# Attention tails turned by TensorE, and an early expert with tiles of its own

## The chip, the cores and the metric

The kernel runs on one core of a Trainium2 chip. The metric is the device time of one execution in microseconds. The kernel before ran three times: 1011.96, 1013.71 and 1017.95 us, a median of 1013.71.

## What is computed

Attention over 8 batches of 8 heads, 576 positions and 64 columns a head. Scores that lie more than tau under their row's maximum count as nothing. Its output, 4608 tokens of 512 columns, goes through a routed layer: a token with a positive skip score is sent to the best of 8 experts, and that expert's result, weighted, is added to it.

```python
scores = scale * np.matmul(q, k.transpose(0, 1, 3, 2))
thresh = np.max(scores, axis=-1, keepdims=True) - tau
scores = np.where(scores >= thresh, scores, -1000000000.0)
attn = np.exp(scores - np.max(scores, axis=-1, keepdims=True))
attn = attn / (np.sum(attn, axis=-1, keepdims=True) + 1e-09)
x = np.matmul(attn, v)                     # then to (4608, 512)
do_compute = x @ w_skip > 0
logits = x[do_compute] @ w_gate;  e_idx = np.argmax(logits, axis=1)
h = np.maximum(xc[mask] @ w1[e], 0.0)      # for each expert e
y[mask] = gate_w[mask, None] * (h @ w2[e])
out = x.copy();  out[do_compute] = xc + y
```

Everything is kept near float32 precision: numbers are split into a high and a low part, and products are made of three matmuls (high by high, high by low, low by high).

## The kernel before

**Attention.** Heads go in 32 pairs. The 576 rows of a head are four blocks of 128 and a tail of 64. A pair has four chunks of two score units each (128 rows by 576 columns) and a ninth unit, M, that holds the tails of both heads, 64 rows and 64 rows. A unit runs as a chain: PE writes scores into one of three PSUM tiles (`sps`, SPB = 3, L522), DVE takes the maximum (L534), ACT makes the threshold (L541) and the exponential (L546), DVE multiplies with the mask (L554), which gives p and frees the PSUM tile. ACT copies p to float16 (L336, "hi"), POOL subtracts to get the low half (L603), and SP issues two DMA transposes of 128-blocks (L608), one of the high and one of the low half. PE multiplies the turned p with v (L643, "AV", tile `avp`). The tail's p (`pm`, one buffer) goes the same way through `hm` and `TM`, five blocks to a transpose instead of nine.

After two chunks and after the tail, ACT copies the AV result to `a`; z, the divisors, is made by DVE (L681, reciprocal L684); POOL scales (L693, L706); PE transposes the result in float32 into the one tile `gps` (GPB = 1, L749), ACT copies it (`xf`), and PE makes the gate's logits (L775; L836 for tails). Every two batches a gate (from L854 on) ranks the tokens of an expert (L938, L939) and POOL scatters the tokens' records into lists (L997).

**What sets the order.** All of this is written out by a list scheduler (class Plan, L77 to L178). Each operation has a key, its place n in the sequence plus an entry of the table OFF (L73), a set of engines with a cost, and dependencies. A ring (`ring.take`, `ring.free`) limits the buffers. Each engine takes, of the operations that are ready by the planner's own costs, the one with the smallest key. The result is one fixed order for each engine; at run time engines wait for each other by semaphores.

**The passage.** One expert, the "early" one, is picked after the last but one batch. While the last attention goes through PE, POOL gathers its tokens (L325), PE transposes them (L1170), ACT and DVE split them into `xh` and `xl` (L1179, L1183), and layer 1 makes eight groups of 12 matmuls (L1204), each followed by ACT's relu (L1207) and DVE's low half (L1210). The four transposes and eight groups all use the tile `gps`. `QK0` and `QK1`, in which `xh`, `xl` and the results lie, use the memory of `hla` and `PTa`. The last logits and tails use score tiles instead. SP reads the lists into `recs` (L1225, L1231).

**The experts.** A loop over jobs (L1611), that is over pieces of an expert's list. For each, POOL gathers tokens from `out` (L325 from L1379), PE transposes them (L1394), makes layer 1 (L1412) and layer 2 (L1474, L1493). Weights are split by ACT (L1374) and by DVE and POOL (L1375). DVE adds the result to the token (L1451), and POOL scatters the rows to `out` (L1452).

Of the kernel before, what the change touches and what calls it, by code (L numbers as in the profile page):

```python
# [73 lines left out]
    ld=1.2, qs=-97.2, S=24.7, mx=-53.4, th=-79.8, e=-1.0, p=-17.9, ph=-22.6, pl=-42.8, tt=40.9, av=108.8, cp=11.0, x=122.9, xw=-26.7, row=49.6, rsp=68.9, init=47.1, L1=20.1, sc=-81.4, d0=88.6, phD=-79.0, v=51.0, vsp=6.9, V2=25.9,  # L74
# [107 lines left out]
def attn_moe_kernel(ctx: ExitStack, tc: tile.TileContext, qq, kk_, vl, vt, tau, wg, w1, w2, out):  # L182
# [43 lines left out]
    XWD = (NFT + NDT) * CAPE  # L226
# [4 lines left out]
    QZs = [a1.tile([P, 2 * S], F32, name=f"QZ{i}") for i in range(QB)]  # L231
    hls = [hla[:, i] for i in range(HLB)]
# [4 lines left out]
    hms = [a1.tile([P, STEP + 1, P], F16, name=f"hm{i}") for i in range(2)]  # L237
# [22 lines left out]
    def settle_m():  # L260
        for hm in hms:
            hv = hm.rearrange("p (a c) n -> p a (c n)", a=2)
            nc.gpsimd.memset(hv[:, :, S:], 0.0)

    ones16 = cp.tile([P, P], BF16, name="ones16")
    linit = cp.tile([P, NB, 2], F32, name="linit")
# [241 lines left out]
    def plan_chunk(g, i):  # L508
# [34 lines left out]
        def expo(u):  # L543
            T["e", g, i, u] = e = ap_.tile([P, 2, HS], F32, name="e", tag="e", bufs=EB)
            c = 2 * i + u
            nc.scalar.activation(e, bank(u), AF.Exp, bias=T["mx", g][:, 0, c : c + 1])  # L546

        def mask(u):
            if M:
                T["p", g, i] = ap_.tile([P, 1, S], F32, name="pm", tag="pm", bufs=1)  # L550
# [24 lines left out]
        for u in units:  # L575
            take = [(ks[0],)] if u else ring.take("pm", 1) if M else ring.take("p", PFB)
# [3 lines left out]
            ks.append(k)  # L580
        if M:
            ring.free("kt", T["Sop", g])
            ring.free("qz", T["Sop", g])
            ring.free("mx", ks)

        def fph():
            if M:
                T["hl", g, i] = hms[g % 2].rearrange("p a b -> p (a b)")
                T["PT", g, i] = TMs[g % 2]
            else:  # L590
                c = NM * g + i
                T["hl", g, i] = hls[c % HLB]
                T["PT", g, i] = PTs[c % PTB]
# [4 lines left out]
        lo0 = (NM + 1) * P if M else w  # L598
# [20 lines left out]
        plan_av(g, i, n, [t0, t1])  # L619

    def plan_av(g, i, n, pt):
# [5 lines left out]
        def av():  # L627
# [22 lines left out]
            n + OFF["av"], av, pt + T["V", b, hp // 2] + T["settle"][1:2] + prev + ([] if prev else ring.take("avp", 1)),  # L650
# [8 lines left out]
    def plan_out(g, i, n):  # L659
        b, hp = divmod(g, HP)  # L660
        M = i == NM
        k = n + OFF["cp"]
# [23 lines left out]
        k = n + OFF["x"]  # L686
        zz = pl.op(k, fz, [x, T["a0"]] + ring.take("z", 4), {DVE: 0.09})
# [35 lines left out]
        k = n + OFF["x"] + 1  # L723
# [37 lines left out]
    def plan_logits(b, hp, k):  # L761
# [3 lines left out]
        t, x = plan_x(k, (b, hp), T["xm", b, hp], lambda t: T["x", b][:, t, hp * P : (hp + 1) * P], last)  # L765
        T["xr", b, hp] = t
        js = []
        for j in range(2):

            def mm(j=j):  # L770
                if j == 0:
                    ps = T["Z", (b, hp)][:, 1] if last else g_tile().rearrange("p a b -> p (a b)")
# [7 lines left out]
            held = [] if last else ring.take("gps", GPB)  # L780
# [12 lines left out]
        ring.free("sps" if last else "gps", [y])  # L793
        if hp == HP - 1:
            if b == B - 2:
                plan_gate(k + 2, pr, 0, NM, [y])
# [20 lines left out]
    def plan_tails(b, k, xtm):  # L817
# [9 lines left out]
        t, x = plan_x(k, ("t", b), xtm, lambda d: T["x2"][:, d * P : (d + 1) * P], last)  # L827
        ring.free("x2", [t, s])
        js = []
        for j in range(2):  # L830

            def mm(j=j):
                if j == 0:
                    T["lvt"] = T["Z", ("t", b)][:, 1, 0:16] if last else g_tile()[:, 0, 0:16]
# [5 lines left out]
            held = [] if last else ring.take("gps", GPB)  # L840
# [8 lines left out]
        ring.free("sps" if last else "gps", [y])  # L849
# [174 lines left out]
    kk = cp.tile([P, 2, E, E], F32, name="kk")  # L1024
# [51 lines left out]
    def plan_early(k, j):  # L1076
# [97 lines left out]
        def xh(d):  # L1174
            if d == 0:
                QKs[:] = [ep.tile([P, XWD], F32R, name=f"QK{i}", tag=f"QK{i}") for i in range(2)]
                j.hh, j.hl = (q[:, 0:nh].rearrange("p (f n) -> p f n", n=CAPE) for q in QKs)
                j.xh, j.xl = (q[:, nh : nh + nx] for q in QKs)
            nc.scalar.activation(j.xh[:, d * CAPE : (d + 1) * CAPE], T["x0", d][:, 0:CAPE], AF.Copy)  # L1179

        def xl(d):
            xs_ = slice(d * CAPE, (d + 1) * CAPE)
# [4 lines left out]
        for a in range(NDT):  # L1187
            t = pl.op(k2 + a, lambda a=a: xt(a), gs + ring.take("gps", GPB), {PE: 0.108 * j.nb})
            q = xo[-2:-1] if a else list(T["last"])
            xo.append(pl.op(k2 + a + 0.1, lambda a=a: xh(a), [t] + q, {ACT: 0.4}))  # L1190
            q = xo[-2:-1] if a else []
            xo.append(pl.op(k2 + a + 0.2, lambda a=a: xl(a), xo[-1:] + q, {DVE: 0.45}))
            ring.free("gps", xo[-1:])
        for f in range(NFT):
# [19 lines left out]
            y = pl.op(k2 + 1 + 0.5 * f, mm, xo[-2:] + hs + ls + ring.take("gps", GPB), {PE: 12 * 0.136})  # L1214
            y = pl.op(k2 + 1.3 + 0.5 * f, hh, [y], {ACT: 0.42})
# [539 lines left out]
```

## Time and profile before

| | value |
|---|---|
| median of 3 runs | 1013.71 us (1011.96 to 1017.95) |
| the profiled execution's own time | 1010.29 us |
| its span, first to last instruction | 1008.5 us |
| mean granted clock of PE | 0.933 of full |
| PE busy | 837.2 us, 83% |
| PE's weight loads (beside the matmuls) | 719.3 us, 71% |
| DVE, ACT, POOL busy | 674.4, 609.9 and 593.4 us |
| DMA queue of transposes, loads and stores | 76.0% of 16 engines' span |

The span has three stages, which the rows below cut at 664 and 732 us. Busy shares are of the whole span; how an engine stands in a stage is seen in the stage's own row. A wait is the idle time of an engine just before an instruction, with what ended it in brackets. [...]

### The profile page before, as it was taken

To read this page: it belongs to the slowest core of one execution; us is meant where nothing else is said; L and a number is where in the kernel's file an instruction comes from. 1 tells how busy PE (TensorE), PEld (TensorE's weight loads), DVE (VectorE), ACT (ScalarE), POOL (GpSimd) and SP (SyncE) were. 2 spreads that over 40 slices of the span, in tenths; PEclk is the share of its full clock that TensorE was granted. 3 is DMA by queue.
4 is the path that set the end of the run, shared out by engine and by line. 5 is a ranking of instruction groups with operands and counts; after the bars stand their busy time and mean duration, and the time that the engine had idled before them with its cause. 6 is when DMAs were issued, how large, how long until landed. Compare 5 with 4: busy or idle time off the path is not lost. (4 is left out here: it accounts for less than half of the span.)

```text
span 1008.5 us, 21609 instructions
## 1 busy us (share of the span) xinstructions
PE 837.2 (83%) x8274; PEld 719.3 (71%) x8274; DVE 674.4 (67%) x1143; ACT 609.9 (60%) x1020; POOL 593.4 (59%) x398
## 2 busy tenths in 40 slices
PE   6788988878889877897988789856697999977985
PEld 5677767757668766776876677645576899967974
DVE  6888878788787787876767878982134565526431
ACT  4778968856787965796886588641123344334430
POOL 3667767748776864686684488763025464445251
PEclk9999999989999997998999899975998999988998
DMA  6999999999999999899999899993046543453420
GB/s 161 185 193 183 190 222 178 195 210 173 177 206 186 199 221 179 152 188 200 172 173 226 162 159 200 158 206 129 2 147 207 188 168 128 152 187 114 160 83 17
DMA packets 387656, 169.89 MB, mean 168 GB/s; under 512 B 354615, under 2 KB 355383, under 8 KB 387552
## 3 DMA queue, kind: packets, MB, share of 16 engines
q1 hardware_dynamic: 382928, 158.35, 76.0%
q0 software_dynamic: 4480, 10.15, 3.1%
q8 instruction: 66, 1.08, 0.4%
q14 instruction: 38, 0.31, 0.1%
q10 hardware_dynamic: 144, 0.00, 0.0%
HBM read 67.76 MB, written 15.21 MB: 82 GB/s over the span
## 5 line engine op out<-in xcount | busy, mean ns | idle before, releaser
L522 PE MATMUL sps<-kt,QZ 128*128 128x288 f32 (+2 forms) x1408 | 353.1, 400 | 70.3 <-DVE p L554 58.8
L603 POOL TENSOR_TENSOR hla<-p,hla 128x1152 f16<-128x1152 f32 x128 | 305.1, 2385 | 162.2 <-ACT hla L336 112.4
L522 PEld LDWEIGHTS sps<-kt,QZ 128*128 128x128 f32 x1408 | 248.9, 201 | 120.6 <-issue 57.4
L534 DVE TENSOR_REDUCE mx<-sps 128x1 f32<-128x576 f32 x288 | 215.3, 752 | 113.3 <-PE sps L522 111.8
L546 ACT ACTIVATE e<-sps,mx 128x576 f32<-128x576 f32 x288 | 205.5, 730 | 29.6 <-DVE mx L534 25.6
L554 DVE SCALAR_TENSOR_TENSOR p<-sps,mx,e 128x576 f32<-128x576 f32 x256 | 197.8, 807 | 13.9 <-POOL hla L603 5.3
L643 PEld LDWEIGHTS <-PTa 128*128 128x128 f16 x3840 | 140.6, 101 | 52.0 <-DMA PTa<-hla 28.9
L643 PE MATMUL avp<-Vh,PTa 128*128 128x65 f16 x2560 | 145.4, 198 | 33.6 <-DMA PTa<-hla 24.5
L336 ACT ACTIVATE hla<-p 128x1152 f16<-128x1152 f32 x128 | 148.5, 1161 | 32.0 <-DVE p L554 15.5
L643 PE MATMUL avp<-Vl,PTa 128*128 128x64 f16 x1280 | 137.5, 196 | 0.0
L541 ACT ACTIVATE mx<-mx,ntau 128x2 f32<-128x2 f32 (+1 forms) x160 | 47.0, 294 | 78.8 <-DVE mx L534 77.1
L1375 POOL TENSOR_TENSOR wl<-wr,wh 128x1024 fp32r<-128x1024 f32 x28 | 72.0, 2589 | 22.8 <-ACT wh L1374 18.3
L1412 PE MATMUL hps<-xh,wh 128*128 128x288 f32 (+4 forms) x224 | 69.1, 308 | 0.1
L1412 PE MATMUL hps<-xl,wh 128*128 128x288 f32 (+4 forms) x224 | 68.0, 304 | 0.0
L1412 PE MATMUL hps<-xh,wl 128*128 128x288 f32 (+4 forms) x224 | 67.8, 303 | 0.0
L1452 POOL DMA_INDIRECT out<-o,ids x20 | 20.0, 1000 | 80.0 <-DVE o L1451 25.1
L1413 ACT ACTIVATE QK<-hps 128x288 fp32r<-128x288 f32 (+4 forms) x56 | 23.9, 426 | 61.0 <-PE hps L1412 60.3
L1374 ACT ACTIVATE wh<-wr 128x1024 fp32r<-128x1024 f32 x60 | 60.6, 1050 | 0.0
L1474 PE MATMUL yps<-wh,QK 128*128 128x512 f32 (+2 forms) x224 | 57.1, 405 | 1.7 <-ACT wh L1374 1.5
L325 POOL DMA_INDIRECT xg<-out,idg x20 | 22.6, 1130 | 60.9 <-issue 33.9
L1375 DVE TENSOR_TENSOR wl<-wr,wh 128x1024 fp32r<-128x1024 f32 x32 | 46.0, 1445 | 9.6 <-ACT wh L1374 9.3
L997 POOL DMA_INDIRECT lst<-rec,si x36 | 35.9, 998 | 25.1 <-DVE si L969 17.9
(236 smaller groups left out, 1285.8 us busy)
## 6 DMA issues: line engine op xcount, KB each, us to landing
wr<-in_w SPq DMA_DIRECT2D x31, 1024.0 KB, 5.5
kt<-in_k SPq DMA_DIRECT2D x32, 288.0 KB, 3.7
QZ<-in_q SPq DMA_DIRECT2D x64, 144.0 KB, 3.3
vraw<-in_vl SPq DMA_DIRECT2D x32, 256.0 KB, 4.7
out<-xb SPq DMA_DIRECT2D x32, 256.0 KB, 3.4
PTa<-hla SPq DMA_TRANSPOSE x256, 3.8
vraw<-in_vt SPq DMA_DIRECT2D x8, 128.0 KB, 4.5
TM<-hm SPq DMA_TRANSPOSE x64, 2.7
```

The source lines that it names most:

```text
L336: nc.scalar.activation(dst, src, AF.Copy)
L522: nc.tensor.matmul(ps[:, j, o : o + w], q[:, at : at + P], k[:, c0 : c0 + w], start=True, stop=True, skip_group_check=True,)
L534: nc.vector.tensor_reduce(T["mx", g][:, 0, c : c + 1], bank(u), AX.XY, ALU.max, negate=True)
L541: nc.scalar.activation(m[:, 1, cs], m[:, 0, cs], AF.Identity, bias=ntau, scale=-1.0)
L546: nc.scalar.activation(e, bank(u), AF.Exp, bias=T["mx", g][:, 0, c : c + 1])
L554: nc.vector.scalar_tensor_tensor(T["p", g, i][:, u].rearrange("p (a b) -> p a b", a=2), bank(u), T["mx", g][:, 1, c : c + 1], T.pop(("e", ...
L603: nc.gpsimd.tensor_tensor(hl[:, lo0 : lo0 + w], T.pop(("p", g, i)).rearrange("p a b -> p (a b)"), hl[:, 0:w], op=ALU.subtract)
L643: nc.tensor.matmul(o[:, 0:e], x[:, w_, cs], y[:, vb, 0:e], start=first and j == 0, stop=kt == NM and j == 2, skip_group_check=True,)
L1374: nc.scalar.activation(w[0][:, sl], rs, AF.Copy)
L1375: lo[q % 2].tensor_tensor(w[1][:, sl], rs, w[0][:, sl].bitcast(F32), op=ALU.subtract)
L1412: nc.tensor.matmul(hp_[:, 0:cap], w_, x, start=(i == 0), stop=(i == len(mm) - 1))
L1474: nc.tensor.matmul(yp[0:m], h, w_, start=(i == 0), stop=(i == len(mm) - 1))
```

## The change

Four things change, and all numbers of the table OFF are new.

1. The tail's p is written in float32 to one of two fixed buffers (`pms`). PE transposes its five blocks in float32 into a score tile; ACT copies that to float16 as the high half, and DVE subtracts to get the low half. This takes the place of ACT's copy, POOL's subtraction and the two DMA transposes of the tail. The turning of a chunk is written after the next chunk's scores.
2. z is made by ACT instead of DVE. The e tiles lie in one fixed buffer.
3. The early expert has `hh0`, `hl0` and `xh0` of its own, its transposes and layer-1 results use the three score tiles, and layer 1 has a key of its own (`L1m`). The last logits and tails use `gps`.
4. A gather is no longer made to wait for scatters of other tokens, nor a scatter for such gathers.

```diff
 ...
-    hms = [a1.tile([P, STEP + 1, P], F16, name=f"hm{i}") for i in range(2)]
+    ea = a1.tile([P, EB, 2, HS], F32, name="ea", tag="EE")
+    hh0, hl0 = (ep.tile([P, NFT, CAPE], F32R, name=f"h0{i}") for i in range(2))
+    xh0 = a1.tile([P, NDT * CAPE], F32R, name="xh0")
+    pms = [a1.tile([P, (NM + 1) * P], F32, name=f"pm{i}") for i in range(2)]
...
+        return lambda: plan_turn(g, i, n, units, ks)
+
+    def plan_turn(g, i, n, units, ks):
+        if i == NM:
+            plan_tail(g, i, n, ks)
+            return
...
+    def plan_tail(g, i, n, ks):
+        def tr():
+            T["X", g] = ps = ps_s.tile([P, 2, 512], F32, name="sps", tag="sps").rearrange("p a b -> p (a b)")
+            for t in range(NM + 1):
+                nc.tensor.transpose(ps[:, t * P : (t + 1) * P], pms[g % 2][:, t * P : (t + 1) * P], ident)
+        def hi(e):
+            T["PT", g, i] = TMs[g % 2]
+            copy(e, T["PT", g, i][:, 0 : NM + 1].rearrange("p a b -> p (a b)"), T["X", g][:, 0 : (NM + 1) * P])
+        def lo():
+            x = T["PT", g, i]
+            nc.vector.tensor_tensor(
+                x[:, NM + 1 :].rearrange("p a b -> p (a b)"),
+                T.pop(("X", g))[:, 0 : (NM + 1) * P],
+                x[:, 0 : NM + 1].rearrange("p a b -> p (a b)"),
+                op=ALU.subtract,
+            )
+        t = pl.op(n + OFF["tt2"], tr, ks + ring.take("sps", SPB), {PE: 1.15})
+        a = pl.op(n + OFF["hi2"], hi, [t] + ring.take("hmT", 2), {ACT: 0.63})
+        c = pl.op(n + OFF["lo2"], lo, [a], {DVE: 0.76})
+        ring.free("pm", [t])
+        ring.free("sps", [c])
+        plan_av(g, i, n, [a, c])
...
-            nc.vector.tensor_scalar(z, T["a", g][:, :, :, D], 1.0e-9, T["s", b], op0=ALU.add, op1=ALU.mult)
+            nc.scalar.activation(z, T["a", g][:, :, :, D], AF.Identity, bias=T["s9", b], scale=T["s", b])
...
-        nx, nh = NDT * CAPE, NFT * CAPE
+        j.hh, j.hl, j.xh = hh0, hl0, xh0
         def half():
-            return g_tile().rearrange("p a b -> p (a b)")
+            return ps_s.tile([P, 2, 512], F32, name="sps", tag="sps")[:, 0]
...
-            t = pl.op(k2 + a, lambda a=a: xt(a), gs + ring.take("gps", GPB), {PE: 0.108 * j.nb})
+            t = pl.op(k2 + a, lambda a=a: xt(a), gs + ring.take("sps", SPB), {PE: 0.108 * j.nb})
...
-            y = pl.op(k2 + 1 + 0.5 * f, mm, xo[-2:] + hs + ls + ring.take("gps", GPB), {PE: 12 * 0.136})
+            y = pl.op(k2 + OFF["L1m"] + 0.5 * f, mm, xo + hs + ls + ring.take("sps", SPB), {PE: 12 * 0.136})
...
         for t in range(j.nb):
             m = j.m(t)
-            gather(j.xg[0:m, t, :], j.idg[0:m, t : t + 1], NTOK)
+            ga = gather(j.xg[0:m, t, :], j.idg[0:m, t : t + 1], NTOK)
+            for x in rows:
+                tc.declare_no_dep(ga.ins, x.ins, reason="every token goes to one expert")
+            gets.append(ga)
...
-        for x in rows:
+        for x in rows + gets:
             tc.declare_no_dep(sc.ins, x.ins, reason="every token goes to one expert")
```

Line numbers below are those of each kernel: the early expert's transposes are L1170 before and L1202 after, its layer-1 matmuls L1204 and L1233.

On DVE, around the end of a pair in the middle of attention, before: `mx` is the maximum of a unit, `p` the mask, `pm` the tail's mask.

```order
L554 SCALAR_TENSOR_TENSOR p<-sps,mx,e 128x576 x2
L554 SCALAR_TENSOR_TENSOR pm<-sps,mx,e 128x576
L534 TENSOR_REDUCE mx<-sps 128x1
L787 COPY lg<-gps 128x64
L534 TENSOR_REDUCE mx<-sps 128x1 x2
L554 SCALAR_TENSOR_TENSOR p<-sps,mx,e 128x576 x2
L681 TENSOR_SCALAR z<-a_111,vmx 128x10
L684 RECIPROCAL z<-z 128x10
```

The same place after the change:

```order
L556 SCALAR_TENSOR_TENSOR pm_116<-sps,mx,ea 128x576
L536 TENSOR_REDUCE mx<-sps 128x1 x2
L716 RECIPROCAL z<-z 128x10
L556 SCALAR_TENSOR_TENSOR p<-sps,mx,ea 128x576 x2
L638 TENSOR_TENSOR TM_118<-sps,TM_118 128x640
L536 TENSOR_REDUCE mx<-sps 128x1 x3
L556 SCALAR_TENSOR_TENSOR p<-sps,mx,ea 128x576 x2
```

The tail's low half (L638) stands between the masks of a later chunk and three maxima; z is gone from DVE.

On PE, at the end of attention, before: the last logits (L775), the rank of the last gate (L938, L939), then the early expert.

```order
L775 MATMUL sps<-wgt,xf 128x16 x2
L938 LDWEIGHTS tri_120
L938 MATMUL gps<-rs_9706,tri_120 128x8
L939 LDWEIGHTS ones_116
L939 MATMUL gps<-rs_9706,ones_116 128x8
...
L1170 MATMUL gps<-ident,xg_9592 128x128 x2
L1170 MATMUL gps<-ident,xg_9592 128x64
L1170 MATMUL gps<-ident,xg_9592 128x128 x2
```

After, the same engine from the last AV matmul on:

```order
L674 MATMUL avp<-Vh_113,TM_119 64x65
L1202 MATMUL sps<-ident,xg_9406 128x128 x2
L1202 MATMUL sps<-ident,xg_9406 128x64
...
L781 MATMUL gps<-ident,x_7567 128x128 x4
L1202 MATMUL sps<-ident,xg_9406 128x128 x2
L1202 MATMUL sps<-ident,xg_9406 128x64
L869 MATMUL gps<-wgt,xf 128x16 x4
L1233 MATMUL sps<-xh_110,wh_9194 128x320
L1233 MATMUL sps<-xl_9500,wh_9194 128x320
L1233 MATMUL sps<-xh_110,wl_9205 128x320
```

The early expert's transposes and four of the eight groups of layer 1 now stand ahead of the rank of the last gate, mixed with the last logits and tails; the other four stand right behind it.

On POOL, late in the loop over jobs, before: L1452 is a scatter, L325 a gather, and brackets name the semaphores that an instruction waits for (DMASW are queue slots of POOL's own transfers).

```order
L1452 DMA out<-o,ids 4608x512 [waits DVE_49]
L325 DMA xg<-out,idg 128x512 [waits DMASW6_49,DMASW7_49,DMASW0_49,DVE_49]
L325 DMA xg<-out,idg 128x512
L325 DMA xg<-out,idg 32x512
L1375 TENSOR_TENSOR wl<-wr,wh 128x1024 [waits DMAHW1_49,Activation_49]
```

After:

```order
L1507 DMA out<-o,ids 4608x512 [waits DMASW0_49,DVE_49]
L327 DMA xg<-out,idg 128x512 [waits DMASW1_49,DVE_49]
L327 DMA xg<-out,idg 128x512 [waits DMASW2_49]
L327 DMA xg<-out,idg 32x512 [waits DMASW3_49]
L1427 TENSOR_TENSOR wl<-wr,wh 128x1024 [waits DMAHW1_49,Activation_49]
```

The place is the same; the gather waits for one slot, used eight transfers before, instead of three that hold the scatters just ahead of it.

## Rows read from the trace of the kernel before

**Rows 1.** The span by stage: length; PE, PEld, DVE, ACT, POOL busy (instructions); clock, DMA share, GB/s.
```profile
7.00:664.00 657.00, 550.30 (x6512) 462.69 (x6511) 523.74 (x845) 493.38 (x824) 452.30 (x270) 0.95 1.01 186
664.00:732.00 68.00, 39.71 (x299) 33.47 (x296) 25.11 (x71) 15.95 (x32) 18.35 (x17) 0.70 0.38 104
732.00:1008.00 276.00, 242.01 (x1444) 217.96 (x1442) 122.00 (x202) 98.29 (x163) 117.74 (x72) 0.94 0.40 142
```

**Rows 2.** Waits of PE from 7 to 664 us: microseconds in total, times, longest.
```profile
PE sps L522 <- DVE p L554: 58.8, 48, 3.9
PE avp L643 <- DMA PTa<-hla: 21.4, 20, 3.0
```

**Rows 3.** Timeline of the passage: start, duration, engine, line, tiles, idle before.
```profile
692.65 1.01 PE L775 MATMUL sps<-wgt,xf 128*128 128x16 f32 x4
...
705.04 0.90 PE L1204 MATMUL gps<-QK,wh 128*128 128x320 f32 x2 [1.05 <-DVE QK L1183]
...
709.12 0.49 DVE L1210 SCALAR_TENSOR_TENSOR QK<-gps,QK 128x320 fp32r<-128x320 f32 x1 [4.13 <-ACT QK L1207]
...
721.42 0.49 DVE L1210 SCALAR_TENSOR_TENSOR QK<-gps,QK 128x320 fp32r<-128x320 f32 x1 [2.58 <-ACT QK L1207]
...
710.03 5.36 SPq L1231 DMA_DIRECT2D recs<-lst  x7
```

**Rows 4.** Waits of PE from 730 to 1009 us.
```profile
PE yps L1493 <- POOL wl L1375: 11.7, 2, 6.4
```

**Rows 5.** Timeline of POOL at 754 us, and of DVE and POOL from 912 to 936.
```profile
754.02 1.06 POOL L325 DMA_INDIRECT xg<-out,idg  x1 [2.60 <-DMA out<-o,id]
...
923.00 1.22 DVE L1375 TENSOR_TENSOR wl<-wr,wh 128x1024 fp32r<-128x1024 f32 x1 [0.41 <-ACT wh L1374]
...
923.89 1.27 POOL L325 DMA_INDIRECT xg<-out,idg  x1 [5.40 <-DMA out<-o,ids]
...
927.03 7.00 POOL L1375 TENSOR_TENSOR wl<-wr,wh 128x1024 fp32r<-128x1024 f32 x3
```

**Rows 6.** Waits of PE from 664 to 732 us.
```profile
PE gps L1204 <- DVE QK L1210: 7.4, 7, 1.1
```

**Rows 7.** Tile xg: operation, count, ns minimum/median/maximum, first and last start.
```profile
L325 POOL DMA_INDIRECT xg<-out,id x3: 957/1007/1066, 679.7 to 682.4; - x3
```

**Rows 8.** DMA issues from 676 to 700 us: count, median us to landing.
```profile
xg<-out,id POOLq DMA_INDIRECT x3, 5.6
```

**Rows 9.** Stretch of 695 to 700 us.
```profile
695.00:700.00 5.00, 2.19 (x8) 1.07 (x8) 3.63 (x27) 0.48 (x2) 0.00 (x0) 0.50 0.00 2
```

**Rows 10.** Timeline, PE at 317 us and DVE at 755 us.
```profile
317.02 0.63 PE L749 MATMUL gps<-ident,xb 128*128 128x128 f32 x4
...
755.53 0.69 DVE L1444 TENSOR_TENSOR QK<-xtp,QK 128x512 fp32r<-128x512 f32 x1 [5.17 <-ACT QK L1443]
```

**Rows 11.** Groups by line and shape: busy us, mean ns, idle before.
```profile
L603 POOL TENSOR_TENSOR hm<-pm,hm 128x576 f16<-128x576 f32 x32 | 41.7, 1303 | 4.1 <-ACT hm L336 4.1
L541 ACT ACTIVATE mx<-mx,ntau 128x2 f32<-128x2 f32 x128 | 37.6, 294 | 71.2 <-DVE mx L534 70.6 <-DVE vki L443 0.4
...
L681 DVE TENSOR_SCALAR z<-a,vmx 128x10 f32<-128x10 f32 x32 | 30.0, 936 | 4.9 <-ACT a L336 4.9
...
L336 ACT ACTIVATE hm<-pm 128x576 f16<-128x576 f32 x32 | 21.4, 670 | 1.8 <-DVE pm L554 1.8
```

**Rows 12.** Tile TM.
```profile
L608 SPq DMA_TRANSPOSE TM<-hm x64: 1200/1247/2872, 32.1 to 675.4; - x64
```

**Rows 13.** The page's costliest groups.
```profile
L522 PE MATMUL sps<-kt,QZ 128*128 128x288 f32 (+2 forms) x1408 | 353.1, 400 | 70.3 <-DVE p L554 58.8
```

**Rows 14.** DMA queues from 100 to 600 us: packets, MB, share.
```profile
q1 hardware_dynamic: 276474, 93.54, 100.6%
```

**Rows 15.** Tile PTa from 100 to 600 us.
```profile
DMA to landing us min/median/max: 3.2/3.7/6.9
```

**Rows 16.** The page's HBM line.
```profile
HBM read 67.76 MB, written 15.21 MB: 82 GB/s over the span
```

More of the change, by code (lines that the diff above doesn't have):

```diff
@@ L543, in expo @@
         def expo(u):
[L544 removed]
+            T["e", g, i, u] = e = ea[:, (STEP * g + 2 * i + u) % EB]
             c = 2 * i + u
@@ L580, in plan_chunk @@
             ks.append(k)
+        T["masks"] = T.get("masks", [])[-2:] + ks
         if M:
@@ L680, in fz @@
             T["z", g] = z = ap_.tile([P, NM + 1, 2], F32, name="z", tag="z", bufs=4)
-            nc.vector.tensor_scalar(z, T["a", g][:, :, :, D], 1.0e-9, T["s", b], op0=ALU.add, op1=ALU.mult)
+            nc.scalar.activation(z, T["a", g][:, :, :, D], AF.Identity, bias=T["s9", b], scale=T["s", b])
         def fr():
             nc.vector.reciprocal(T["z", g], T["z", g])
-        k = n + OFF["x"]
-        zz = pl.op(k, fz, [x, T["a0"]] + ring.take("z", 4), {DVE: 0.09})
+        k = n + OFF["x"] - late_
+        zz = pl.op(k, fz, [x, T["a0"]] + ring.take("z", 4), {ACT: 0.2})
         zz = pl.op(k + 0.1, fr, [zz], {DVE: 0.11})
@@ L778, in mm @@
                     )
-            held = [] if last else ring.take("gps", GPB)
+            held = ring.take("gps", GPB)
             js.append(pl.op(k + 1 + 0.5 * j, mm, [x, T["init"]] + (held if j == 0 else js), {PE: 0.43}))
@@ L792, in plan_logits @@
         T["lgo", b] = y = pl.op(k + 1.8, lg, deps, {DVE: 0.135})
-        ring.free("sps" if last else "gps", [y])
+        ring.free("gps", [y])
         if hp == HP - 1:
             if b == B - 2:
+                k -= OFF["eg"]
                 plan_gate(k + 2, pr, 0, NM, [y])
@@ L838, in mm @@
                     )
-            held = [] if last else ring.take("gps", GPB)
+            held = ring.take("gps", GPB)
             js.append(pl.op(k + 1 + 0.5 * j, mm, [x, T["init"]] + (held if j == 0 else js), {PE: 0.43}))
@@ L848, in plan_tails @@
         T["lgt", pr] = y = pl.op(k + 1.8, lg, js + [T["lgo", b - 1]], {DVE: 0.1})
-        ring.free("sps" if last else "gps", [y])
+        ring.free("gps", [y])
     cnt_op = []
@@ L1174, in xh @@
         def xh(d):
[L1175 to L1178, printed above, removed]
             nc.scalar.activation(j.xh[:, d * CAPE : (d + 1) * CAPE], T["x0", d][:, 0:CAPE], AF.Copy)
         def xl(d):
+            if d == 0:
+                j.xl = a1.tile([P, NDT * CAPE], F32R, name="xl0", tag="EE")
             xs_ = slice(d * CAPE, (d + 1) * CAPE)
@@ L1292, in op @@
             return pl.op(k, lambda: None, deps, eng, lat=lat)
-        hs = [op([T["w2"][q // 2]], {ACT: 0.947}) for q in range(4)]
-        ls = [op([x], {DVE: 1.135}) for x in hs]
+        hs = [op([T["w2"][q // 2]] + [(y,) for y in T["hh"]], {ACT: 0.947}) for q in range(4)]
+        ls = [op([x] + [(y,) for y in T["L1"]], {DVE: 1.135}) for x in hs]
         x = op([T["list"]] + [(y,) for y in ls], {DVE: 0.2})
@@ L1354, in attn_moe_kernel, with tile @@
     ps_y = moe.enter_context(tc.tile_pool(name="ps_y", bufs=3, space=PSUM, reuse_waits="tile"))
-    late = moe.enter_context(tc.tile_pool(name="late", bufs=1))
+    class late:
+        at, base = 0, None
+        @classmethod
+        def tile(cls, shape, dt, name):
+            if cls.base is None:
+                cls.base = ep.tile([P, NFT * CAPE], F32, name="lateb", tag="h00")
+            n = int(np.prod(shape[1:]))
+            x = cls.base[0:1, cls.at : cls.at + n]
+            cls.at += n
+            if len(shape) == 3:
+                return x.rearrange("p (a b) -> p a b", a=shape[1])
+            if len(shape) == 4:
+                return x.rearrange("p (a b c) -> p a b c", a=shape[1], b=shape[2])
+            return x
     tab = cp.tile([1, 2 * NOV + 1], I32, name="tab")
@@ L1359, in attn_moe_kernel @@
     rows = []
+    gets = []
+    QKs[:] = [ep.tile([P, NFT * CMAX], F32R, name=f"QK{i}", tag=f"QK{i}") for i in range(2)]
     def split_w(src, raws=(), lo=(nc.vector, nc.gpsimd)):
```

72 lines of the change are left out of this document (36 added, 36 removed).

## The prediction

> **What bounds the kernel now.** I read the table of stages first. It cuts the span into attention (7 to 664 us), the passage from attention to the experts (664 to 732) and the experts (732 to 1008) [rows 1]. In attention PE is busy 550 of 657 us at a mean clock of 0.95, DVE 524, ACT 493, POOL 452, and the DMA share is 1.01: four engines are loaded between 69 and 84%, none is full. In the passage PE is busy 40 of 68 us at a clock of 0.70 and every other engine less: that stretch is a chain of dependent steps. In the experts PE is busy 242 of 276.
>
> Next, PE's own waits in attention [rows 2]: 58.8 us for a score tile that DVE's mask still reads, 21.4 us for transposed p to land. The first is the ring of three score tiles, the second the way over DMA. Then the passage by instructions [rows 3]: logits until 693.66, layer 1 of the early expert from 705.04, then one of its eight groups every 3.07 us ((721.42 - 709.12) / 4). Last, PE's wait in the experts for the low halves of the weights [rows 4], and on POOL the gathers ahead of these halves [rows 5].
>
> **The early expert (first term).** Before, its four transposes and eight groups of 12 matmuls share one PSUM tile and stand behind the last gate. Of the 3.07 us of a group PE waits 7.4/7 = 1.06 us for DVE to empty the tile [rows 6]. With three tiles PE writes the next one meanwhile, so a group costs it 3.07 - 1.06 = 2.01 us, and eight cost 16.1.
>
> The start moves too: transposes and layer 1 stand right behind the last AV matmuls, ahead of the last rank. The three gathers that they need are issued by 682.4 + 1.0 and land 5.6 us after issue, about 689 [rows 7, 8]. I take 690 for the start. To the 16.1 us come 3 for logits, tails and rank that are now mixed in (three groups of four small matmuls, 1.01 us each at half clock [rows 3]), and 3.2 for a start at half clock. The granted clock is 0.50 from 695 to 700 [rows 9], and the first group, begun in that state, took 709.12 - 705.04 = 4.08 us from its first matmul to DVE's reading, where a later one takes about 2.5 (3.07 less DVE's 0.49 and some 0.08 until PE starts again). That is 1.58 a group; I count two. End: 690 + 16.1 + 3 + 3.2 = 712.3. Before, the eighth group ends three periods after the fifth, 721.42 + 3 x 3.07 - 0.5 = 730.1. The difference is 17.8; I take **-18**. Bounds: no group at half clock, -21; all eight, six more by 1.58 = 9.5 later, -8.
>
> Layer 2 is let follow as before. What could be late next is the gather of the first listed job, which needs the lists: SP issues their reads until 710.03 + 5.36 = 715.4 [rows 3], about when layer 1 is now done, and layer 2 lies between that gather and its use.
>
> From 695 to 700 PE had float32 transposes and small gate matmuls, at a granted 0.50 [rows 9], and attention, which holds four float32 transposes per pair already, a mean of 0.95 [rows 1]. [...]
>
> **Gathers (second term).** POOL's gather of a job waits for the scatter of the job before, which writes other tokens. The gather at 923.89 sat 5.40 us for it, and three low halves of weights queue behind it, from 927.03 [rows 5]. DVE's first half starts at 923.00, when ACT's first piece is there; ACT needs about 1 us for the next, so POOL could start near 924: 3.1 us earlier, 3.5 with the gathers' slack. Of this pattern there are three; at the other two the same working gives 4.2 each. PE waits 11.7 us for such halves at two of them [rows 4], so the gain reaches it. The first gather of the loop, at 754.02, sat 2.60, and PE waits for what it brings. Sum 3.5 + 4.2 + 4.2 + 2.6 = 14.5; since PE may meet its next wait sooner, I take **-13**. Bounds: 0, if queue slots or lists hold the gathers instead; -18, the three waits of PE (11.7, and about 4 at the third) with the 2.6.
>
> **Attention (third term).** Per pair, 32 times:
> - PE: four float32 transposes take 0.63 us [rows 10], so the five that are added 0.78, in all 25 us. PE is idle 657 - 550 = 107 us of this stage, so a part falls into waits: I count half, +12. Best 0, worst +25.
> - PE's wait for transposed p: ten DMA transposes per pair become eight, and the tail's AV needs no DMA. Of the 21.4 us and some 6 that I add for the tail's own, half goes: **-14**.
> - POOL: the low half of the tail goes, 41.7 us [rows 11]. POOL is idle a third of the stage, so alone it is worth nothing.
> - ACT: the copy of 576 columns goes (0.67 each), one of 640 comes, 0.67 x 640/576 = 0.74, and z comes, priced like the nearest small row at 0.29 [rows 11]: 32 x 0.36 = +12 on 493. Hidden in its 164 us of idle time; if not, +12 is inside the bounds.
> - DVE: z goes, 30.0 us [rows 11] (a mean with stalls in it), and the low half of 640 columns comes, 0.69 x 640/512 = 0.86 [rows 10], 27.6: about -2.
> - SP: 64 issues of 1.25 us go, 80 us of its queue [rows 12]; what this is worth is rival 1.
> - Score ring: nine allocations a pair become ten. The tile is held for transposes, ACT's and DVE's copy, 0.78 + 0.74 + 0.86 = 2.4 us and latencies. Nothing, if that falls beside other units; at worst PE loses a score unit per pair, 353.1/288 = 1.23 us [rows 13], 39 us.
>
> The added DVE step stands between two masks and the transposes behind the first scores of the next pair, so PE and DVE have other work around them; that cover is why I take 0 for the ring. Sum: +12 - 14 = **-2**, bounds +40 (about PE's worst and half the ring) and -40 (rival 1).
>
> For a larger gain speaks the queue with the transposes: 100.6% of 16 engines' time [rows 14]. Against it, a transpose lands 3.2/3.7/6.9 us after issue (minimum, median, maximum) [rows 15], so no backlog grows, and HBM moves 82 GB/s over the span [rows 16]. [...]
>
> **Sum.** -18 - 13 - 2 = -33. The profiled execution took 1010.3 us (span 1008.5 and 1.8 around it), which gives 977.3. The median of the runs lies 3.4 above that execution: **980**. Own range 966 to 994: first two terms between -39 and -8, not both at one end, attention 10 either way.
>
> **Rivals.**
> 1. The transposes' queue, or SP that issues into it, paces attention. A pair has 72 blocks of other transposes and 10 of the tail's: 10/82 of 657 us is 80, half of it 40. 980 - 38 = 942. For it: the share in rows 14 and the 80 us of SP. Against: rows 15, and that PE's longest wait is for the mask. Chance 0.13.
> 2. PE pays in full. For it: PE is the most loaded engine, and its order is fixed, so a transposition that waits for a late mask holds up the scores behind it. Attention +20: 980 + 22 = 1002, still faster. Against: the 107 us of idle time. Chance 0.15.
> 3. The passage gains little, because layer 2 or the first listed job meets a new wait (lists, weights, clock): first term -5, gathers -6, attention +10. 1013.7 - 1 = about 1013. For it: the lists come no earlier. Against: layer 1's groups lose their wait wherever they stand. Chance 0.08.
> 4. Slower: the tenth tile in the ring of three. Each pair loses a score unit, 1.23, on top of the 0.78: 32 x 2.01 = 64, less the 31 of the first two terms, 1013.7 + 33 = 1047. From 31/32 = 0.97 us per pair on, the kernel is slower. For it: the 58.8 us of rows 2 are a wait for this ring. Against: it is one tile in ten, emptied by copies and not by the chain of maximum, exponential and mask. Chance 0.09.
>
> Forecast 0.55. Times of this kernel can be told apart from about 0.5% on, 5 us. Faster: 0.55 + 0.13 + 0.15 = 0.83; same 0.08; slower 0.09. The range 946 to 1008 leaves out rivals 3 and 4 and half of rival 1, about 0.2.
>
> **What would show it.** Right, if layer 1's groups stand about 2 us apart and end near 712, gathers follow scatters without the 5 us, PE's waits for POOL's halves go below 2 us each, and attention keeps its length within 10 us. The ring shows as PE's wait for score tiles far above 59 us; the queue as an attention some 40 us shorter; rival 2 as PE's busy time up by 25 with its waits unchanged. I am wrong if attention moves by more than 15 us, or if the clock stays at 0.5 through layer 1.

## The result and the profile after

The changed kernel takes 938.66 us, the median of four runs (935.18 to 942.50), against 1012.84 for the kernel before beside it: a ratio of 0.927, with an interval of 0.921 to 0.933. The forecast was 980, with a range of 946 to 1008: the sign was right, the size was not, and the time lies under the range. The profiled execution has a span of 935.8 us, 72.7 less than before.

Three marks divide that: the start of the last AV matmul (685.6 before, 649.2 after), the first matmul of layer 2 of the early expert (731.59 and 679.03), and the end.

| | before | after | difference | forecast |
|---|---|---|---|---|
| attention, to the last AV | 685.6 | 649.2 | -36.4 | -2 |
| passage, to layer 2 | 46.0 | 29.8 | -16.2 | -18 |
| experts, to the end | 276.9 | 256.8 | -20.1 | -13 |

The stretches of the changed kernel, with the columns of [rows 1]:

```profile
7.00:649.00 642.00, 559.48 (x6821) 481.47 (x6820) 533.56 (x863) 511.62 (x869) 426.51 (x247) 0.97 0.94 180
649.00:679.00 30.00, 24.14 (x142) 21.63 (x139) 10.38 (x48) 8.72 (x20) 7.42 (x9) 0.82 0.29 103
679.00:935.00 256.00, 238.21 (x1444) 214.67 (x1444) 139.43 (x202) 98.64 (x163) 120.03 (x73) 0.97 0.45 153
```

and attention of the kernel before, cut at its own last AV:

```profile
7.00:686.00 679.00, 562.18 (x6670) 473.55 (x6669) 537.65 (x865) 500.65 (x837) 464.24 (x279) 0.94 1.01 189
```

PE was given 160 transposes (23.0 us) and is still busy 3 us less, at a mean clock of 0.97 instead of 0.94; its idle time fell from 116.8 to 82.5 us. Its waits in the changed kernel, which answer to [rows 2], from 7 to 645 us:

```profile
PE sps L524 <- DVE p L556: 53.7, 50, 3.4
PE avp L674 <- DMA PTa<-hla: 6.3, 10, 1.7
```

The wait for turned p fell from 21.4 to 6.3 us. The wait for the score ring is no longer than before (58.8), so the tenth tile did not do the harm that rival 4 feared; a smaller cost can't be ruled out by this row, since other things changed with it.

The passage, PE's timeline after, which answers to [rows 3]:

```profile
653.44 0.48 PE L1202 MATMUL sps<-ident,xg 128*128 128x128 f32 x1 [4.02 <-DMA xg<-out,id]
654.30 2.60 PE L1202 MATMUL sps<-ident,xg 128*128 128x128 f32 x8 [0.39 <-DMA xg<-out,id]
656.83 1.12 PE L781 MATMUL gps<-ident,x 128*128 128x128 f32 x4
657.74 0.93 PE L1202 MATMUL sps<-ident,xg 128*128 128x128 f32 x3
658.64 1.89 PE L869 MATMUL gps<-wgt,xf 128*128 128x16 f32 x8
660.37 0.61 PE L1233 MATMUL sps<-xh,wh 128*128 128x320 f32 x1
660.78 0.47 PE L1233 MATMUL sps<-xl,wh 128*128 128x320 f32 x1
661.04 0.47 PE L1233 MATMUL sps<-xh,wl 128*128 128x320 f32 x1
...
666.98 0.31 PE L1233 MATMUL sps<-xh,wl 128*128 128x320 f32 x1
667.13 0.30 PE L1233 MATMUL sps<-xh,wh 128*128 128x320 f32 x1
...
677.25 0.31 PE L1233 MATMUL sps<-xh,wl 128*128 128x320 f32 x1
679.03 4.04 PE L1529 MATMUL yps<-wh,h 128*128 128x512 f32 x16 [1.47 <-ACT wh L1426]
```

Layer 1 runs from 660.37 to 677.56, 17.2 us instead of 25, with no wait between groups. The matmuls stand 0.26 us apart in the first group and 0.15 later: one group at half clock (granted 0.52 from 660.0 to 663.6 us and 1.00 from there to 677.56), where two were counted. It starts 11 us after the last AV and not 4 as assumed. The wait of 4.02 us for the gathered tokens was foreseen. Behind it stand 4.0 us of the tokens' own transposes (L1202), at a mean granted clock of 0.51 from 653 to 660, and 3.0 us of logits and tails (L781, L869).

### The profile page after: what moved, and what is told of

Same layout as the page of the kernel before. It is cut to its first block, busy times and chain, and to the rows that moved or that the text cites. A ratio compares the mean times of both kernels' runs of the same rounds, so it can differ in the third digit from the quotient of the medians.

```text
span 935.8 us, 21710 instructions
## 1 busy us (share of the span) xinstructions
PE 827.0 (88%) x8434; PEld 722.9 (77%) x8434; DVE 686.9 (73%) x1140; ACT 621.2 (66%) x1054; POOL 559.2 (60%) x367
## 5 line engine op out<-in xcount | busy, mean ns | idle before, releaser
L524 PE MATMUL sps<-kt,QZ 128*128 128x288 f32 (+2 forms) x1408 | 340.8, 392 | 59.6 <-DVE p L556 53.7
L524 PEld LDWEIGHTS sps<-kt,QZ 128*128 128x128 f32 x1408 | 245.1, 196 | 107.8 <-issue 44.3
L548 ACT ACTIVATE ea<-sps,mx 128x576 f32<-128x576 f32 x288 | 207.7, 731 | 27.4 <-DVE mx L536 15.9
L556 DVE SCALAR_TENSOR_TENSOR p<-sps,mx,ea 128x576 f32<-128x576 f32 x256 | 196.6, 810 | 14.0 <-ACT mx L543 10.9
L674 PEld LDWEIGHTS <-PTa 128*128 128x128 f16 x3840 | 135.8, 100 | 21.8 <-DMA PTa<-hla 9.6
L674 PE MATMUL avp<-Vh,PTa 128*128 128x65 f16 x2560 | 139.8, 196 | 10.9 <-DMA PTa<-hla 7.9
L674 PE MATMUL avp<-Vl,PTa 128*128 128x64 f16 x1280 | 132.8, 194 | 0.0
L1427 DVE TENSOR_TENSOR wl<-wr,wh 128x1024 fp32r<-128x1024 f32 x32 | 52.1, 1642 | 7.9 <-ACT wh L1426 7.8
L487 POOL TENSOR_TENSOR Vl<-vraw,Vh 128x1024 f16<-128x1024 f32 (+1 forms) x23 | 44.6, 1939 | 9.4 <-ACT Vh L338 9.3
L1469 DVE SCALAR_TENSOR_TENSOR QK<-hps,QK 128x288 fp32r<-128x288 f32 (+4 forms) x56 | 26.4, 471 | 32.4 <-ACT QK L1468 32.2
```

The costliest lines, as they stand in the source:

```text
L487: (nc.gpsimd if e == POOL else nc.vector).tensor_tensor(T["Vl", b][:, ts], vraw[:, ts], Vh[:, ts, 0:D], op=ALU.subtract)
L524: nc.tensor.matmul(ps[:, j, o : o + w], q[:, at : at + P], k[:, c0 : c0 + w], start=True, stop=True, skip_group_check=True,)
L556: nc.vector.scalar_tensor_tensor(T["p", g, i][:, u].rearrange("p (a b) -> p a b", a=2), bank(u), T["mx", g][:, 1, c : c + 1], T.pop(("e", ...
L674: nc.tensor.matmul(o[:, 0:e], x[:, w_, cs], y[:, vb, 0:e], start=first and j == 0, stop=kt == NM and j == 2, skip_group_check=True,)
L1427: lo[q % 2].tensor_tensor(w[1][:, sl], rs, w[0][:, sl].bitcast(F32), op=ALU.subtract)
```

## The experiments

Each ran beside the kernel before; ratios are to that, and the last AV's start is from the one profiled execution of each. That execution can lie some microseconds from the run's median: 8.0 above it in x3 (969.54 us), 6 to 7 below it in x11 and x15, 4.5 below it in x6. Differences in the last column are uncertain by as much. The diffs show the lines that matter and not the whole edits.

```
run                       us       ratio (interval)        last AV
before                    1010-1013                        685.6
after                     938.66   0.927 (0.921 to 0.933)  649.2
x1_tail_by_dma            985.75   0.968 (0.962 to 0.975)  695.4
x3_old_table              961.58   0.948 (0.946 to 0.951)  678.9
x15_old_table_urgent      964.38   0.954 (0.950 to 0.957)  682.9
x4_z_on_dve               963.98   0.952 (0.950 to 0.955)  672.8
x4c_z_reduce_on_dve       934.50   0.924 (0.920 to 0.929)  651.0
x2_idle_dma               967.35   0.955 (0.953 to 0.957)  678.9
x6_idle_dma_small         961.13   0.953 (0.949 to 0.958)  668.7
x11_idle_plain_dma        958.93   0.949 (0.943 to 0.956)  664.2
x7_before_z_on_act        1000.48  0.991 (0.987 to 0.994)  671.7
x8_before_no_tail_dma     990.83   0.983 (0.978 to 0.988)  663.0
x9_before_both            973.45   0.961 (0.954 to 0.968)  649.0
x5_before_gathers         989.65   0.978 (0.972 to 0.984)  687.3
x10_one_transpose         943.81   0.933 (0.927 to 0.939)  657.6
x12_loads_on_pool         955.89   0.944 (0.940 to 0.949)  670.4
x13_loads_on_act          956.93   0.946 (0.942 to 0.950)  666.1
x14_stores_on_pool        947.16   0.936 (0.933 to 0.940)  655.7
```

### The tail's way, and the order

x1 gives the changed kernel the tail's old way, x3 the old table. z stays on ACT in both, and the turning of a chunk stays behind the next chunk's scores.

```diff
 # x1_tail_by_dma, in plan_tail
+        a = pl.op(n + OFF["ph"], fph, ks + ring.take("hm", 2), {ACT: w / 1200 + 0.12})
+        c = pl.op(n + OFF["pl"], fpl, [a], {POOL: w * 0.00208 + 0.1})
+        t0 = pl.dma(n + OFF["tt"], lambda: turn(0), [a] + ring.take("hmT", 2), [nb * 8 * 0.0193], 0.3)
 # x3_old_table: the numbers of before in OFF, and
+    tt2=95.0, hi2=-20.0, lo2=5.2, eg=0.0, L1m=1.0, ex=0.0, eav=0.0,
```

> The changed kernel, but the tail's p is turned as before (ACT's float16 copy, POOL's low half, two DMA transposes); table, z on ACT, early expert and gathers stay as changed, and the tail's float16 copies lie in the memory that the early expert's results use later. The last AV matmul ended at 685.9 us before and 649.4 after. Theory A, the way of the tail (transposes on SP's queue, landing, POOL's work): all of the 36 us come back, attention ends near 685, time near 975. Theory B, the new order (the table and the chunk turned one later): attention stays within 10 us of 649, time 938 to 950. Both in part: between.

> The changed kernel with the table of before for every entry that both have; the new entries are tt2 = 95, hi2 = -20, lo2 = 5.2, L1m = 1, and no shift at the end (eg, ex and eav 0). Theory B (the order is what gained): attention back near 680 to 690 and a later layer 1, time 975 to 990. Theory A (the tail's way): attention within 10 us of 649, time 938 to 955. Rival 2 or 4 of the forecast (PE or the score ring pay for the transposes unless the order hides them): attention longer than before, above 700.

Neither theory alone holds. With the tail on DMA the changed kernel ends attention 9.8 us later than the kernel before (695.4 against 685.6); with the old table it keeps 6.7 of the 36.4 us, and some more if x3's profiled execution is put right by its median. But z on ACT is in both, and that is worth something by itself. The like comparison is with x7 below, which has the old order, the tail on DMA and z on ACT (671.7). From there the new order alone makes attention 23.7 us longer (x1), PE's transposes alone do not shorten it beyond the noise (x3, 678.9), and both together shorten it by 22.5 (649.2). An order is worth something only for the way it was made for.

### DVE's z

```diff
 # x4_z_on_dve
-            nc.scalar.activation(z, T["a", g][:, :, :, D], AF.Identity, bias=T["s9", b], scale=T["s", b])
+            nc.vector.tensor_scalar(z, T["a", g][:, :, :, D], 1.0e-9, T["s", b], op0=ALU.add, op1=ALU.mult)
 # x4c_z_reduce_on_dve
+            nc.vector.tensor_reduce(z, T["a", g][:, :, :, D : D + 1], AX.X, ALU.add)
```

> The changed kernel with z made by DVE again; the order of all other instructions stays. z on DVE took 936 ns in the mean before, 32 times, with a reciprocal of similar size at 206 ns, so some 23 us of it are stalls. Theory C (DVE's stalls in z gave a large part of the 36 us): 10 to 23 us slower, 949 to 962. Theories A and B: within 4 us of the changed kernel.

> The changed kernel with z made on DVE at the same place as in x4_z_on_dve, but by a sum over one element instead of the addition and product with the scale (left out: the scale of the values and the 1e-9). Theory C1 (that form of z waits on DVE until POOL's running subtraction is over; it did so in x4_z_on_dve, 1111 ns in the mean against 220 at least): the sum over one element takes about 0.2 us each time, and the time is within 6 us of the changed kernel, 935 to 945. Theory C2 (the place itself: DVE waits there for ACT's copy of the AV result, and the masks behind wait with it): 955 to 966 as x4_z_on_dve.

x4 lost 25 us, x4c nothing, although both put an instruction of 128 x 10 at the same place of DVE. Tile z in x4 and then in x4c (ns minimum, median, maximum):

```profile
L713 DVE TENSOR_SCALAR z<-a,vmx x32: 216/590/2398, 49.5 to 673.8; 128x10 f32<-128x10 f32 x32
```

```profile
L713 DVE TENSOR_REDUCE z<-a x32: 149/160/169, 51.1 to 653.9; 128x10 f32<-128x10 f32 x32
```

What it waits for could have been read from the kernel before. DVE around 250 us, and then POOL there:

```profile
249.45 2.72 DVE L681 TENSOR_SCALAR z<-a,vmx 128x10 f32<-128x10 f32 x1
252.09 0.75 DVE L534 TENSOR_REDUCE mx<-sps 128x1 f32<-128x576 f32 x1
```

```profile
248.50 2.40 POOL L603 TENSOR_TENSOR hla<-p,hla 128x1152 f16<-128x1152 f32 x1
250.82 1.30 POOL L603 TENSOR_TENSOR hm<-pm,hm 128x576 f16<-128x576 f32 x1
```

z starts inside one POOL subtraction and ends at 252.17, just behind the next one (252.12). It is no single case: 13 of the 32 z of the kernel before took more than 0.35 us, and 18 of those of x4, and every one of them ended within 0.05 us behind the end of a `tensor_tensor` of POOL. Four of the 13 ended behind the second of two such instructions in a row. In x4c no z took more than 0.17 us at the same place. What makes the difference between the two instructions no run shows.

### What each is worth on the kernel before

```diff
 # x7_before_z_on_act: z as after, in the order of before
+            nc.scalar.activation(z, T["a", g][:, :, :, D], AF.Identity, bias=T["s9", b], scale=T["s", b])
 # x8_before_no_tail_dma
         def turn(j):
+            if M:
+                return
 # x9_before_both: x7 and x8
```

> The kernel before with z made by ACT; the order of all other instructions stays. Theory C (DVE's stalls in z, 23 us in all, lie on the path of attention): 10 to 23 us faster than before, 990 to 1003. Theory D (the gains of the parts exist only together with an order that uses them): within 5 us of before, 1007 to 1017.

> The kernel before without the tail's two DMA transposes per pair (left out: the tail's AV multiplies zeros instead of p); ACT's copy and POOL's low half of the tail stay, and the order of all that is left. Theory A1 (load of SP and the queue): 20 to 36 us faster, 977 to 993. Theory D (worth it only with an order that uses it): at most 10 us faster, 1002 to 1013.

> The kernel before with both edits of x7 and x8: z on ACT, and no DMA transposes of the tail (left out: the tail's AV multiplies zeros). x7 measured -12 us and x8 -21. If the two are separate costs on the path of attention: -33, time 975 to 983. If they hide behind each other: -21 to -25, time 987 to 992.

In attention z gave 13.9 us, the tail's transposes 22.6, both 36.6 (11.8, 21.4 and 37.0 by the medians of the whole time): they add up, and to what the change gained there (36.4). In x8 this is PE's wait for turned p, 8.2 us instead of 21.4, and PE's busy time, which fell by 10.5 us for the same matmuls at a clock of 0.95 instead of 0.94. PE's wait in x8 and its attention in the columns of [rows 1]:

```profile
PE avp L647 <- DMA PTa<-hla: 8.2, 9, 2.3
```

```profile
7.00:663.00 656.00, 551.68 (x6673) 466.30 (x6673) 532.12 (x872) 499.56 (x836) 465.97 (x302) 0.95 0.94 179
```

x9 does none of PE's transposes, ACT's new copy and DVE's low half (it keeps ACT's old copy and POOL's low half of the tail); the changed kernel does all of them and ends attention at the same place. So the new order makes up for them. That is not the same as hiding them: PE's wait for masks is longer in the changed kernel (53.7 us) than in x9,

```profile
PE sps L524 <- DVE p L556: 43.5, 43, 4.4
```

and other waits are shorter. How much the new order would gain without these steps no run shows. The old order doesn't make up for them: x3 ends 29.9 us behind x9, or some 23 if the medians of their times are taken less the time behind the last AV. x15 tried other places for the tail's three steps in the old table:

```diff
-    tt2=95.0, hi2=-20.0, lo2=5.2,
+    tt2=60.0, hi2=-45.0, lo2=-50.0,
```

> As x3_old_table, but with the tail's three steps more urgent: tt2 = 60, hi2 = -45, lo2 = -50 instead of 95, -20 and 5.2. If the 30 us of attention in x3 are the price of PE's and DVE's added work in an order not made for it: again 955 to 968. If they came from my choice of the three entries: 935 to 948.

By its time it is no better than x3, so it isn't that choice of entries alone; other choices were not tried. Its last AV can't be compared, since layer 1 of the early expert stands ahead of it there (from 664.59 us on). Attention of x9 and of x3, in the columns of [rows 1], shows how the price is paid:

```profile
7.00:649.00 642.00, 551.02 (x6673) 466.12 (x6673) 511.33 (x841) 507.90 (x867) 466.23 (x302) 0.95 0.97 183
```

```profile
7.00:679.00 672.00, 573.71 (x6827) 489.98 (x6825) 539.59 (x864) 514.28 (x868) 425.76 (x248) 0.95 0.90 175
```

From x9 to x3 PE is busy 22.7 us more, just its transposes, and idle 7 us more. From x9 to the changed kernel it is busy 8.5 more, at a clock of 0.97, and idle 8.5 less.

### What a transpose on SP's queue costs

x2, x6 and x11 add idle transfers to the changed kernel that nobody waits for in attention. They use the memory of the early expert's results, whose first relu therefore waits for the end of attention. That costs nothing: from the last AV to the end it is 286 to 287 us in all three and in the changed kernel.

```diff
 # x2_idle_dma, in hi and in lo of plan_tail
+            nc.sync.dma_start_transpose(sinks[:, 2 * g % 8], spare)
 # x6_idle_dma_small
+            nc.sync.dma_start_transpose(sinks[:, 2 * g % 8, 0:1], spare[:, 0:P])
 # x11_idle_plain_dma, two for each
+            for h in range(2):
+                nc.sync.dma_start(sinks[:, 2 * g % 8, h, 0:64], spare[:, 0:64])
```

> The changed kernel with two more DMA transposes per pair of five blocks each, from a tile of zeros into a spare tile, that nobody waits for; they stand on SP where the tail's high and low half are done. So SP's issues and the blocks in the queue are those of before, while PE still turns the tail. Every other engine's order is that of the changed kernel. Theory A1 (rival 1: the load on SP and on the queue set the pace): 25 to 36 us slower, time 965 to 975. Theory A2 (the wait of the tail's AV and POOL's work, not the load) and theory B (the order): within 5 us of the changed kernel, 934 to 944.

> As x2_idle_dma (the changed kernel with two idle DMA transposes per pair), but each turns one block instead of five. SP still issues 64 more transposes; the queue gets 64 more blocks instead of 320. Theory A1a (the queue's blocks cost the 29 us of x2_idle_dma): about a fifth, 4 to 10 us, time 942 to 949. Theory A1b (SP's issue time, some 1.2 us each, holds back the transposes that AV waits for): nearly all of it, 20 to 30 us, time 959 to 969.

> As x6_idle_dma_small (the changed kernel with idle transfers on SP), but four small plain copies per pair instead of two transposes; a plain transfer holds SP about 0.5 us, so the four hold it about 2.0 us per pair, against 2.4 there. Theory A1b (SP's time to issue is what costs): 15 to 22 us slower, time 954 to 961. Theory A1c (something of transposes themselves in the queue): within 6 us of the changed kernel.

A fifth of the blocks keeps 19.5 of the 29.7 us in attention, and plain copies that hold SP nearly as long keep 15.0; by the medians of the whole time it is 22.5 and 20.3 of 28.7. What comes back is PE's wait for the turned p of the chunks, 6.3 us in the changed kernel, here from 7 to 660 us in x2, x6 and x11:

```profile
PE avp L678 <- DMA PTa<-hla: 25.2, 27, 2.7
PE avp L678 <- DMA PTa<-hla: 23.5, 20, 2.5
PE avp L680 <- DMA PTa<-hla: 16.7, 21, 1.9
```

So most of it is SP's time to issue, and the blocks in the queue are the lesser part. SP in the kernel before, which the page's list of engines leaves out, 298 to 320 us:

```profile
298.54 2.07 SPq L608 DMA_TRANSPOSE TM<-hm  x1
300.70 2.75 SPq L608 DMA_TRANSPOSE PTa<-hla  x2
303.54 1.25 SPq L608 DMA_TRANSPOSE TM<-hm  x1
304.89 5.59 SPq L608 DMA_TRANSPOSE PTa<-hla  x4
310.58 1.21 SPq L364 DMA_DIRECT2D QZ<-in_q  x2
311.84 0.58 SPq L359 DMA_DIRECT2D kt<-in_k  x1
312.54 3.58 SPq L608 DMA_TRANSPOSE PTa<-hla  x2
316.21 2.58 SPq L608 DMA_TRANSPOSE TM<-hm  x2
318.89 1.32 SPq L608 DMA_TRANSPOSE PTa<-hla  x1
```

Each issue starts about 0.1 us after the one before: SP is full here. Summed over its records from 50 to 640 us, it issues for 521 of 590 us in the kernel before, for 463 in the changed kernel, and for 523 to 528 in x2, x6 and x11. Its pauses of more than 0.2 us sum to 32 us before and to 98 in the changed kernel. A landing is counted from the issue, so a full SP doesn't show in it: its median was 3.7 us before and 3.8 in the changed kernel, while PE's wait for turned p fell from 21.4 to 6.3. The transposes were late before they were issued.

### Three tries to relieve SP further, and the gathers

```diff
 # x10_one_transpose: one of 18 blocks where the second of nine stood
+            nc.sync.dma_start_transpose(T["PT", g, i][:, 0 : 2 * nb], T["hl", g, i][:, 0 : 2 * lo0])
 # x12_loads_on_pool (x13_loads_on_act: nc.scalar)
+            (nc.gpsimd if g > 1 else nc.sync).dma_start(T["k", g], kk_[g])
+                (nc.gpsimd if g > 1 else nc.sync).dma_start(q[h * D : h * D + D, h * S : h * S + S], qq[g][h * D : h * D + D])
 # x14_stores_on_pool
+                nc.gpsimd.dma_start(out[r0 : r0 + P, :], T["x", b][:, t, :])
```

> The changed kernel, but the high and the low half of a chunk are turned by one DMA transpose of 18 blocks instead of two of nine, where the second stood. A transpose of one block held SP 1.23 us, of five 1.29 and of nine 1.34, so SP should save some 1.2 us 128 times, about 150 us of its queue. Theory A1b: faster than the changed kernel by 5 to 25 us, 914 to 934, unless the high half's later start makes AV wait. Theory A1a (the blocks in the queue): no faster than 934, and slower if the high half is late.

> The changed kernel, but from the third pair on the loads of k and q (three per pair, 0.58 us each on SP) are issued by POOL instead of SP, in the same places of the order. 1.75 us per pair leave SP. x11 put 2.4 us per pair on it (four at 0.60) and cost 15 us in attention. If SP still bounds: 8 to 15 us faster, 924 to 931. If PE bounds now: within 5 us of 939. If POOL, on which each takes about 1 us and waits for PE to be done with the buffer, holds up its low halves: slower, 945 to 965.

> As x12, but ACT issues the loads. SP bounds and ACT has room: 924 to 931. PE bounds: 934 to 944. ACT is busy three quarters of attention and DVE's masks hang on its exponentials, so if an issue takes 0.6 us there and waits for buffers in ACT's order: 945 to 970.

> The changed kernel, but attention's results are stored by POOL, which made them, instead of SP (32 and 16 issues, some 0.45 us each, about 21 us of SP's queue). If SP bounds: 3 to 6 us faster, 932 to 936. Otherwise within 4 us of the changed kernel, or slower by what POOL's issues take (48 at 1 us) if its low halves are late.

None beats the changed kernel. x10 can't be told from it by the intervals, and its reason was wrong: a transpose of 18 blocks held SP 3.25 us in the median, more than two of nine in the changed kernel (1.34 each; tile PTa, 100 to 600 us):

```profile
L615 SPq DMA_TRANSPOSE PTa<-hla x102: 2407/3248/4818, 101.0 to 599.9; - x102
```

x12 to x14 are slower by 8 to 18 us. A load took POOL 0.56 us in the median (x12) and a store 0.57 in the mean (x14), not the 1 assumed. On POOL the loads wait for their buffers ahead of the low halves, and the masks behind those; x12's waits of POOL, then of DVE (1.7 in the changed kernel):

```profile
POOL QZ L366 <- PE sps L524: 12.7, 6, 4.7
```

```profile
DVE p L556 <- POOL hla L608: 10.1, 9, 5.0
```

So after the change SP is no longer the engine to relieve at any price. For POOL the rows of x12 show what the loads disturb; why x13 and x14 lost is not shown. It also means that x2, x6 and x11, which add work, may contain some cost of a disturbed order; x8 and x9 only take work away from attention.

```diff
 # x5_before_gathers, on the kernel before
+            for x in rows:
+                tc.declare_no_dep(ga.ins, x.ins, reason="every token goes to one expert")
```

> The kernel before, where gathers and scatters of different tokens no longer wait for each other; nothing else changes. The forecast's second term: -13 us, time 996 to 1003. From the start of layer 2 of the early expert to the end it took 276.9 us before and 256.8 after: if the gathers alone make the 20 us, time 990 to 995; if a part comes with the rest of the change (the expert's own buffers, the planned order of its first weights), 996 or more.

From layer 2 to the end x5 takes 256.5 us, like the changed kernel: the gathers alone make the whole gain of that stage. POOL in x5, at the place of [rows 5]:

```profile
911.20 0.99 POOL L1456 DMA_INDIRECT out<-o,ids  x1 [0.17 <-issue]
912.50 2.30 POOL L325 DMA_INDIRECT xg<-out,idg  x1 [0.31 <-DVE ej L1591]
...
916.14 7.09 POOL L1376 TENSOR_TENSOR wl<-wr,wh 128x1024 fp32r<-128x1024 f32 x3
```

## Why the prediction was wrong

**The step that failed is the third term**, "Sum: +12 - 14 = -2", where -36 was measured. It mis-sized what z cost, what the tail's transposes cost beyond the wait, and what PE would pay.

1. *DVE: "z goes, 30.0 us (a mean with stalls in it) ... about -2".* The new low half (26.1 us of busy time) was set against z, as if DVE's busy time were the cost. z's 30 us were 7 of work (32 at 0.22, the shortest) and 23 of standing still, in the middle of a chain that PE waits for. Taking z away gave 13.9 us (x7). What the new low half costs by itself no run separates. The row hinted at it: a mean of 936 ns for an instruction of ten columns.
2. *Waits for transposed p: "half goes: -14".* As a wait this was nearly right: it fell by 13.2 us in x8 and by 15.1 in the changed kernel. But the tail's transposes were worth 22.6 us (x8); the rest is PE's busy time, which fell with the waits and which no entry had. The reason was wrong as well. No row shows PE waiting for the tail's transposes to land; what it waited for were the chunks' transposes, held up by SP. SP's time I named in rival 1, gave 0.13, and argued away with landing times and HBM rate. Neither sees a full issuing engine. The rows of SP itself decide (521 of 590 us), and I hadn't read them.
3. *PE: "I count half, +12".* In the new order nothing is left of it at the end of attention: x9 without the transposes and the changed kernel with them end within 0.2 us. In the old order PE is busy the full 23 longer (x3 against x9), which was rival 2.

Rival 1 had nearly the right size (-40, 942 us) by a mechanism that holds for 23 of the 36 us. Rival 4, a kernel made slower by the score ring, with PE's wait far above 59 us, is refuted by its wait of 53.7 us.

**The first term was right in size** (-18 forecast, -16.2 measured), in part by luck, since two errors nearly cancel: the start 7 us later behind the last AV than assumed, layer 1 itself 5 us shorter (17.2 against 16.1 + 3 + 3.2). Of the 7 us, 4.0 are the tokens' own transposes, which the sum had left out, and 3.0 the logits and tails, which it had placed inside layer 1. That layer 1 starts at half clock, and for two groups, was my estimate from [rows 3] and [rows 9]; the run showed one such group, and what sets the clock no run shows. This reading is from the timeline; no run changes the passage alone.

**The second term had the right mechanism and was too small**: -13 forecast, -20.4 measured (x5). In x5, PE's waits in the experts fell from 23.4 to 7.4 us, 16.0 where the sum had 14.5 and I cut it. The other 4 us are PE's matmuls themselves, 242.0 to 237.9 us, at a granted clock of 0.97 instead of 0.94; no term had that, and why the clock rose no run shows.

The sum's own bounds for attention, +40 and -40, contain the -36.4. The range left them out: it was cut at 946, which left half of rival 1 outside, and rival 1 was the only place where -40 had a chance.

## What to carry to other kernels

Read the engine that issues the transfers like any other: here SP's list had next to no gaps (521 of 590 us), while a median landing of 3.7 us and 82 GB/s of HBM gave no sign of it. A mean that lies far above the median of the same small instruction (936 and 243 ns for z) can be a stall; look for the other engine's instruction that ends with it, and price its removal by the stall. Where a static order is written by a planner, a change of the work and a change of the order must be judged together: here, with z on ACT in all cases, the new order alone lost 24 us, the new work alone gained nothing beyond the noise, and both gained 22.5.

## What the runs showed of the hardware

- A DMA transpose held SP 1.23 us for one block (x6), 1.25 to 1.29 for five (the tail's before, and x2), 1.34 for nine, and 3.25 for 18 (x10), all medians: nearly flat up to nine, then more than twice.
- A `tensor_scalar` of 128 x 10 on DVE took 216 to 2720 ns (x4 and the kernel before); all 31 that took more than 350 ns ended within 0.05 us behind the end of a `tensor_tensor` of POOL, four of the 13 of the kernel before behind the second in a row. A `tensor_reduce` of the same size took 149 to 169 in the same place (x4c).
- Five float32 transposes of 128 x 128 took PE 23.0/32 = 0.72 us per pair, and the mean clock of attention didn't fall with 160 more of them (0.94 before, 0.97 after). Behind the last AV the granted clock was 0.51 from 653 to 660 us, where PE made transposes and small gate matmuls. PE had also waited 4.02 us just before. What made the clock fall these rows can't tell.
